# Constants folded into the small matrices, one read of the first batch, and a due time for every operation

## The chip, the cores and the metric

The kernel runs on one core of one Trainium2 chip. The metric is the device time of one execution in microseconds (us). The median of three runs is 2964.1 us (2961.46 to 2966.37).

## The reference, cut to what matters

Two batches of 12480 rows of 128 numbers go through an attention with 32 inducing rows, and then through two dense layers with a hidden width of 2048. All is float32; the weights arrive as float64 and are narrowed on the chip.

```python
def mab(q, kv):
    s = scale * (q @ kv.T);  a = exp(s - s.max(-1));  a /= a.sum(-1) + 1e-9
    return a @ kv
h   = mab(inducing, x)          # 32 x 128 per batch
x   = mab(x, h)                 # 24960 x 128 over both batches
h   = x @ w_in;  h2 = h*h;  h3 = h2*h                       # layer 1
g   = (a[0] + a[1]*h + a[2]*h2 + a[3]*h3) / (1 + |b[0]|*|h| + |b[1]|*h2 + 1e-6)
x   = g @ w_out
h   = x @ w_in2;  out = (h * cos(h)) @ w_out2               # layer 2
```

## The kernel before, in words

A batch is cut into 26 blocks of 480 rows, so there are 52 blocks. The last product of the attention, `a @ h`, is never formed: since a row of x after the attention is a row of `a` (32 numbers) times `h`, layer 1 multiplies `a` by `h @ w_in`, a small matrix that `plan_product` makes once per batch. To keep float32 precision in TensorE's faster float32r form, each small matrix is held as a rounded upper half and the rest (hi and lo). There are three of them for each of the eight tiles `k` of 256 hidden columns: `mst` (h @ w_in), `m3` (times a[3]) and `m1` (times a[1]).

Layer 1 of a tile (`moe1_tile`), for each of two halves of 128 hidden columns: `mmA` gives h; ScalarE takes `sq` (L859) and `ab` (L862); GpSimd makes the denominator with `wq` (L865) and `qq` (L868), over both halves at once; ScalarE takes `ln` (L871) and `ex` (L874), which is 1/Q; GpSimd's `ee` (L877) prepares a correction of it. For the numerator `mmX` writes a[3]*h into a PSUM bank; VectorE's `n1` (L883) adds a[2] and multiplies by h squared; `mmY` adds a[1]*h into the same bank; VectorE's `gr` (L891) adds a[0] and multiplies by 1/Q; `ng` (L896) applies the correction; `mmB` (L901) multiplies by `w_out`. `mmA`, `mmX` and `mmY` all show as L853.

Layer 2 (`moe2_tile`), sixteen times per block: `mmC` (L984), `rk` on ScalarE (L987, to an integer), `rd` on VectorE (L990), `sn` on ScalarE (L993, the sine), `gg` on VectorE (L996), `mmD` (L999). Layer 2 of a block runs while layer 1 of the next is under way. Logarithm and exponential live in one ScalarE table and the sine in another; `phases` lets the `ln`/`ex` of one block and the `sn` of the block before it alternate as wholes, with a table load between (L1079).

The order of the instructions on every engine is written out by a planner at build time. Each operation has a cost, dependencies, buffers to take and give back, and a priority; `Plan.order` simulates the engines and takes the ready operation with the lowest priority each time. Before, the priority is `16*block + slope*k` plus one offset for each kind of operation (`OFF`; `START` for the first two blocks).

Ahead of the blocks, `plan_attention` reads the rows of a batch twice from HBM, in 26 pieces of 240 KB each time: once to transpose them for the scores (L558, L498) and once for `a @ x` (L664), and it narrows the weights (`plan_narrow`, pieces of 384 columns): one ScalarE operation (L402), four VectorE ones (L406, L414, L420, L426) and three on GpSimd (L432, L436, L437), the last two a mask for values near zero. The attention of the second batch runs among the first two blocks; block 2 and later wait for all of it (`full`). Where the second batch begins (block 26), `plan_product` has to overwrite the small matrices of the first.

Of the kernel before, what the change touches and what calls it, by code (L numbers as in the profile page):

```python
# [21 lines left out]

OWN = {"act": 140.0, "dve": 115.0, "pool": 125.0}
HOPS = {("act", "dve"): 142.0, ("dve", "act"): 128.0, ("act", "pool"): 170.0}
# [5 lines left out]
    "ADDED": (0, 1, 2, 3, 4, 5, 6, 7),  # L30
    "OFF": {
# [12 lines left out]
        "mmY": -1100207.547, "mmB": 572.571, "mmC": 263.586, "mmD": 459.524, "sq": -1101114.205, "ab": 352.265, "ln":  # L44
        565.602, "ex": -1099842.388, "rk": 515.904, "sn": -1101113.631, "wq": -1099913.759, "qq": -177.405, "ee":
        -1100601.458, "wb": -1099292.294, "n0": -1099927.018, "n1": 356.455, "gr": -1099724.394, "ng": 299.344, "rd":
        -197.362, "gg": 1101720.214, "cpx": -57.339,
# [27 lines left out]
class Op:  # L75
    __slots__ = ("eng", "cost", "fn", "prio", "phase", "acq", "rel", "lat", "ndep", "users", "seq", "ready", "t0", "key", "main", "lock", "after", "inst", "tag", "deps")

    def __init__(self, eng, cost, fn, deps, prio, phase=None, acq=(), rel=(), lat=0.0, key=None, main=False, lock=None, tag=None):
        self.eng, self.cost, self.fn, self.prio = eng, cost, fn, prio
        self.phase, self.acq, self.rel, self.lat = phase, acq, rel, lat  # L80
        self.key, self.main, self.lock, self.tag = key, main, lock, tag
        self.users = []
        self.after = []
        self.inst = None
        self.ready = 0.0
        deps = [d for d in deps if d is not None]
        self.deps = deps
        self.ndep = len(deps)
        for d in deps:
            d.users.append(self)  # L90


class Plan:
# [3 lines left out]
    def __init__(self, pools, phases, switch=1300.0):  # L97
# [64 lines left out]
    def order(self):  # L162
# [6 lines left out]
        clock = Clock()  # L169
        events = []  # L170
# [13 lines left out]
        while events:  # L184
# [12 lines left out]
            for e in engines:  # L197
# [37 lines left out]
                if e == "pe":  # L235
                    cost = clock.run(now, cost)
# [23 lines left out]
def kernel(  # L260
# [19 lines left out]
    G = 4  # L280
# [8 lines left out]
    TINY = math.ldexp(1.125, -15) ** 2  # L289
# [3 lines left out]
    ROOM = [['xn', 'x1', 'xn', 'x1', 'x2', 'xn', 'x2'], ['xn']]  # L293
    PEPRIO = [0.0, 0]
    OFF, START = TUNE["OFF"], TUNE["START"]
    APRIO = [-1000000.0, OFF["ap1"]]
    WPRIO = [OFF["wp0"], OFF["wp1"], OFF["wp2"], OFF["wp3"]]
    ADDED = TUNE["ADDED"]
    PARTS = TUNE["PARTS"]
    NAT = 2  # L300
# [17 lines left out]
    m3 = {k: const.tile([128, 256], F32R, name=f"m3_{k}") for k in ADDED}  # L318
    m1 = {k: const.tile([128, 256], F32R, name=f"m1_{k}") for k in ADDED}
# [17 lines left out]
    plan = Plan({"slot": 3, "hc": TUNE["NX"]["hc"], "accB": 1, "accD": 1, "at": NAT, "xt": 2, "pk": 2, "ot": 1, "on": 2, "xn": NXN, **NX, "x1": NX["x1"] + 1, "x2": NX["x2"] + 1}, phases)  # L337
# [26 lines left out]
    XT = [t[:, 0:TB] for k in ("x5", "x6", "ot", "on") for t in M[k]]  # L364
    late = [(k, len(M[k])) for k in ("x5", "x6", "ot", "on")]
    for k, n in (("x3", 4), ("x2", 2)):
        late.append((k, n))
        XT += [M[k][i][:, h * TB:(h + 1) * TB] for i in range(n) for h in range(2)]
    XT = XT[:NQ]
# [27 lines left out]
    def plan_narrow(n, load, tiles, dst, prio, deps, acq=(), rel=()):  # L397


        def sq():  # L400
            raw, a, _ = tiles()
            nc.scalar.activation(out=a, in_=raw[:, :, 1].bitcast(F32), func=AF.Square)  # L402

        def mant():
            raw, _, _ = tiles()
            nc.vector.tensor_scalar(  # L406
                out=dst().bitcast(I32), in0=raw[:, :, 1], scalar1=0x07FFFFFF, scalar2=3,
                op0=ALU.bitwise_and, op1=ALU.logical_shift_left,
            )

        def top():
            raw, _, _ = tiles()
            d = dst().bitcast(I32)
            nc.vector.scalar_tensor_tensor(  # L414
                out=d, in0=raw[:, :, 1], scalar=-0x40000000, in1=d, op0=ALU.bitwise_and, op1=ALU.bitwise_or
            )

        def power():
            _, _, b = tiles()
# [4 lines left out]
        def rest():  # L424
            raw, _, b = tiles()
# [4 lines left out]
        def both():  # L430
            _, _, b = tiles()
# [9 lines left out]
        o1 = op("act", 94 + 0.833 * n, sq, [ld], prio, main=main)  # L441
        o2 = op("dve", 68 + 1.04 * n, mant, [ld], prio, main=main)
        for fn, t in ((top, 1.2), (power, 0.62), (rest, 1.12)):
            o2 = op("dve", 68 + t * n, fn, [o2], prio, main=main)
        o2 = op("pool", 95 + 2.16 * n, both, [o2], prio, main=main)
        return op("pool", 220 + 4.4 * n, keep, [o1, o2], prio, rel=rel, main=main)

    def plan_weights(w, out, dst, prio):

        ends = []  # L450
        for f in range(0, DFF, 384):
            n = min(384, DFF - f)
# [9 lines left out]
            def tiles(c=c, d=d, n=n):  # L462
                raw = M["x3"][c["x3"]][:, 0:2 * n].bitcast(I32).rearrange("p (n w) -> p n w", w=2)
                t = M["x1"][d["x1"]]
                return raw, t[:, 0:n], t[:, n:2 * n]
# [650 lines left out]
```

## Time and profile before

| | |
|---|---|
| median of three runs | 2964.1 us |
| the profiled execution | 2961.48 us, its span 2959.7 us |
| PE, DVE, ACT, POOL busy | 96%, 90%, 93%, 81% |
| granted clock of TensorE, mean | 0.985 |
| read from HBM, written | 33.97 MB, 12.78 MB |

A span is the time from the first to the last instruction. Engine names: PE is TensorE, DVE VectorE, ACT ScalarE, POOL GpSimd, SP the engine that issues the DMAs. L883 is line 883 of the kernel. An instruction's duration can overlap the next one's, so the distance of two starts (a slot) is often shorter than the duration.

### The profile page before, as it was taken

The page shows a single profiled execution, that of the slowest core. Times are in us where ns is not written, and L with a number is a line of the kernel's source. Part 1 is how long each engine was busy: PE and PEld are TensorE (multiplying, and loading weights), DVE is VectorE, ACT ScalarE, POOL GpSimd, SP SyncE. Part 2 cuts the span into 40 slices and gives each one's busy share as a digit, 9 for nine tenths or more (in the row PEclk, how much of TensorE's full clock was granted, in tenths as well). Part 3 has the DMA queues.
Part 4 walks back from the last instruction along what each step waited for, and adds up shares of the span by engine and source line. Part 5 has one row for each costly group of instructions (what it writes and reads, how often), then busy time and mean ns, then how long its engine had stood idle before and what let it go on. Part 6 is the DMA issues. An engine that isn't in the chain of part 4 may idle for free.

```text
span 2959.7 us, 31027 instructions
## 1 busy us (share of the span) xinstructions
PE 2837.3 (96%) x8903; PEld 1462.6 (49%) x8903; DVE 2654.1 (90%) x4444; ACT 2752.6 (93%) x4701; POOL 2390.8 (81%) x1392
## 2 busy tenths in 40 slices
PE   6789999999999999999989999999999999999999
PEld 3345455554555545555444455454554545545454
DVE  6889999899998999989989989899898998989987
ACT  3689999999999999999989999999999999999995
POOL 5799788787887878878768878788787887878871
PEclk8789999999999999999999999999999999999999
DMA  9420000000000000000000000000000000000000
GB/s 252 136 74 4 4 7 4 7 4 4 7 4 7 4 4 7 4 8 4 4 7 4 4 7 4 4 7 4 7 4 4 7 4 7 4 4 7 4 7 7
DMA packets 27585, 48.75 MB, mean 16 GB/s; under 512 B 3028, under 2 KB 7412, under 8 KB 27412
## 3 DMA queue, kind: packets, MB, share of 16 engines
q1 hardware_dynamic: 27412, 46.76, 5.7%
q8 instruction: 70, 1.15, 0.2%
q14 instruction: 103, 0.84, 0.1%
HBM read 33.97 MB, written 12.78 MB: 16 GB/s over the span
## 4 chain that ended last, share of the span: by engine, by line
PE 70%; DVE 20%; ACT 5%; issue 3%; DMA 1%; POOL 1%; SPq 0%; DVEq 0%; ACTq 0%; POOLq 0%
PE acc L999 20%; PE bank L984 17%; PE bank L853 16%; PE acc L901 14%; DVE bank L891 5%; DVE x L896 5%; DVE bank L883 4%; DVE x L990 3%; PE bank L1025 1%; DVE x L996 1%; ACT x L871 1%; ACT x L874 1%; PE bank L812 1%; DMA x<-in_moe_w_in_dram 1%; ACT x L987 1%
## 5 line engine op out<-in xcount | busy, mean ns | idle before, releaser
L877 POOL TENSOR_TENSOR x<-x,x 128x960 f32<-128x960 f32 x315 | 703.6, 2250 | 360.7 <-ACT x L874 360.1
L853 PE MATMUL bank<-at,m 128*128 128x480 f32 x1664 | 775.8, 521 | 12.1 <-DVE x L896 4.1
L883 DVE SCALAR_TENSOR_TENSOR bank<-bank,par,x 128x480 f32<-128x480 f32 x832 | 592.5, 720 | 205.8 <-PE bank L853 195.8
L984 PE MATMUL bank<-xt,wt 128*128 128x480 f32 x1664 | 746.9, 571 | 0.3 <-ACT xt L957 0.2
L999 PE MATMUL acc<-x,wt 128*128 128x480 f32 x1664 | 744.8, 566 | 0.0
L868 POOL TENSOR_TENSOR x<-x,x 128x960 f32<-128x960 f32 x315 | 705.3, 2246 | 4.8 <-ACT x L862 3.9
L901 PE MATMUL acc<-x,wout 128*128 128x480 f32 x1460 | 703.7, 569 | 0.0
L993 ACT ACTIVATE x<-x 128x480 f32<-128x480 f32 x832 | 487.5, 614 | 59.5 <-DVE x L990 53.3
L990 DVE TENSOR_TENSOR x<-x,bank 128x480 f32<-128x480 int32 x832 | 524.9, 646 | 14.5 <-ACT x L987 11.7
L996 DVE TENSOR_TENSOR x<-x,bank 128x480 f32<-128x480 f32 x832 | 518.3, 648 | 10.9 <-PE acc L999 1.7
L891 DVE SCALAR_TENSOR_TENSOR bank<-bank,par,x 128x480 f32<-128x480 f32 x716 | 503.7, 717 | 11.4 <-PE bank L853 10.1
L987 ACT ACTIVATE x<-bank 128x480 int32<-128x480 f32 x832 | 465.7, 599 | 25.7 <-PE bank L984 23.8
L853 PEld LDWEIGHTS bank<-at,m 128*128 128x128 f32 x1664 | 307.4, 190 | 351.5 <-DVE bank L883 121.3
L859 ACT ACTIVATE x<-bank 128x480 f32<-128x480 f32 x832 | 448.6, 594 | 21.9 <-PE bank L853 17.1
L862 ACT ACTIVATE x<-bank,babs 128x480 f32<-128x480 f32 x730 | 465.7, 700 | 0.0
L984 PEld LDWEIGHTS bank<-xt,wt 128*128 128x128 f32 x1664 | 302.9, 189 | 324.9 <-issue 143.2
L896 DVE SCALAR_TENSOR_TENSOR x<-x,bank 128x480 f32<-128x480 f32 x730 | 458.7, 645 | 5.2 <-POOL x L877 1.1
L999 PEld LDWEIGHTS acc<-x,wt 128*128 128x128 f32 x1664 | 315.4, 190 | 276.1 <-issue 255.0
L853 PE MATMUL bank<-at,mst 128*128 128x480 f32 x832 | 375.0, 492 | 54.6 <-DVE x L896 46.5
L865 POOL TENSOR_SCALAR x<-x,babs 128x960 f32<-128x960 f32 x358 | 384.3, 1081 | 15.7 <-ACT x L859 15.5
L874 ACT ACTIVATE x<-x 128x960 f32<-128x960 f32 x358 | 358.9, 1043 | 0.2
L871 ACT ACTIVATE x<-x 128x960 f32<-128x960 f32 x315 | 319.1, 1035 | 3.3 <-POOL x L868 2.8
(125 smaller groups left out, 2415.2 us busy)
## 6 DMA issues: line engine op xcount, KB each, us to landing
wide<-in_x_dram SPq DMA_DIRECT2D x75, 240.0 KB, 3.9
out_dram<-on SPq DMA_DIRECT2D x52, 240.0 KB, 2.4
x<-in_x_dram SPq DMA_DIRECT2D x29, 240.0 KB, 7.8
x<-in_moe_w_in_dram SPq DMA_DIRECT2D x10, 384.0 KB, 6.5
x<-in_moe_w_out_dram SPq DMA_DIRECT2D x10, 384.0 KB, 5.1
x<-in_moe_w_in_dram SPq DMA_DIRECT2D x2, 128.0 KB, 4.3
x<-in_moe_w_out_dram SPq DMA_DIRECT2D x2, 128.0 KB, 4.2
ind<-in_inducing_dram SPq DMA_DIRECT2D x1, 16.0 KB, 1.6
```

What stands on the lines that cost most here:

```text
L853: return nc.tensor.matmul(out=ps(e), lhsT=m[k][:, h * 128:(h + 1) * 128], rhs=M["at"][at["at"]], **flags)
L868: nc.gpsimd.tensor_tensor(out=fl("x1"), in0=fl("x2"), in1=fl("x1"), op=ALU.add)
L877: nc.gpsimd.tensor_tensor(out=fl("x1"), in0=fl("x1"), in1=fl("x2"), op=ALU.mult)
L883: nc.vector.scalar_tensor_tensor(out=ps(cx[h]), in0=ps(cx[h]), scalar=par[:, 2:3], in1=hf("x3", h), op0=ALU.add, op1=ALU.mult)
L891: nc.vector.scalar_tensor_tensor(out=ps(cx[h]), in0=ps(cx[h]), scalar=par[:, 0:1], in1=hf("x2", h), op0=ALU.add, op1=ALU.mult)
L896: nc.vector.scalar_tensor_tensor(out=hf("x1", h), in0=hf("x1", h), scalar=-2.0, in1=ps(cx[h]), op0=ALU.add, op1=ALU.mult)
L901: nc.tensor.matmul(out=acc[0][:, 0:TB], lhsT=wout1[:, (2 * k + h) * C:(2 * k + h + 1) * C], rhs=hf("x1", h), start=(k == 0 and h == 0), st ...
L984: return nc.tensor.matmul(out=ps(), lhsT=win2[:, f * 128:(f + 1) * 128], rhs=M["xt"][xc["xt"]], start=True, stop=True)
L987: nc.scalar.activation(out=fl("x5").bitcast(I32), in_=ps(), func=AF.Identity, bias=0.25)
L990: nc.vector.tensor_tensor(out=fl("x5"), in0=fl("x5").bitcast(I32), in1=ps(), op=ALU.subtract)
L996: return nc.vector.tensor_tensor(out=fl("x6"), in0=fl("x5"), in1=ps(), op=ALU.mult)
L999: nc.tensor.matmul(out=acc[1][:, 0:TB], lhsT=wout2[:, f * C:(f + 1) * C], rhs=fl("x6"), start=first, stop=last)
```

## The change

Five things change. (1) `a[2]` and `a[0]` are added to the entries of `m3` and `m1` when these are made (the weights of an attention row sum to one), so `n1` and `gr` become plain products. The product is made twice per tile, once for `mst` and once for `m3` and `m1`, and the two wait for different predecessors; the lower halves of `m3` and `m1` are made on POOL. (2) The rows of batch 0 are read once, 15 pieces of 7 rows per partition, into buffers of layer 1, and serve both passes. (3) Weights are narrowed in 32 pieces of 256 columns, without the two mask operations; the last addition is on DVE. The weights of layer 2 are loaded into buffers that come free after batch 0's second pass. [...] (5) The copies of the attention weights (`cpe`) move from DVE to ACT.

```diff
+    def due(blk, name, i=0, early=0.0):
+        if blk < 2 and name in START:
+            return START[name] + START["block"] * blk + START["tile"] * i * (1.0 if name in SINGLE else 0.5)
+        return PERIOD * blk + TAU[f"{name}{i}"] + ATT["origin"] - early
...
         def n1(h):
-            nc.vector.scalar_tensor_tensor(
-                out=ps(cx[h]), in0=ps(cx[h]), scalar=par[:, 2:3], in1=hf("x3", h), op0=ALU.add, op1=ALU.mult
-            )
+            return nc.vector.tensor_tensor(out=ps(cx[h]), in0=ps(cx[h]), in1=hf("x3", h), op=ALU.mult)
...
         def gr(h):
-            nc.vector.scalar_tensor_tensor(
-                out=ps(cx[h]), in0=ps(cx[h]), scalar=par[:, 0:1], in1=hf("x2", h), op0=ALU.add, op1=ALU.mult
-            )
+            nc.vector.tensor_tensor(out=ps(cx[h]), in0=ps(cx[h]), in1=hf("x2", h), op=ALU.mult)
...
-    def plan_product(b, k, oh, p, ends):
+    def plan_product(b, k, oh, p, ends, stage):
-        before = [blocks[b * NQ - 1][n][k] for n in ("rA", "rX", "rY") if k in blocks[b * NQ - 1][n]] if b else []
+        prev = blocks[b * NQ - 1] if b else {}
+        before = [prev[n][k] for n in (("rA",) if stage == 0 else ("rX", "rY")) if prev]
...
-        def hj(m, s):
-            nc.scalar.activation(out=m, in_=bank[c["half"]][:, 0:256], func=AF.Identity, scale=s)
-        def lj(m, s):
-            return nc.vector.scalar_tensor_tensor(
-                out=m[64:128], in0=bank[c["half"]][64:128, 0:256], scalar=s[64:128], in1=m[64:128].bitcast(F32),
-                op0=ALU.mult, op1=ALU.subtract,
-            )
+        def line(i):
+            if ON["line"] == "act":
+                return nc.scalar.activation(
+                    out=whole[i], in_=bank[c["half"]][:, 0:256], func=AF.Identity, scale=par[:, 3 - 2 * i:4 - 2 * i],
+                    bias=par[:, 2 - 2 * i:3 - 2 * i],
+                )
+        def hj(i):
+            nc.scalar.activation(out=(m3, m1)[i][k], in_=whole[i], func=AF.Copy)
+        def lj(i):
+            m = (m3, m1)[i][k]
+            nc.gpsimd.tensor_tensor(out=m[64:128], in0=whole[i][64:128], in1=m[64:128].bitcast(F32), op=ALU.subtract)
...
+        if b == 0:
+            for i, (k, t) in enumerate(NATURAL):
+                n = min(LG, NJ - LG * i)
+                if n > 0:
+                    dst = M[k][t][:TP, 0:n * C].rearrange("p (g c) -> p g c", g=n)
+                    def ld(dst=dst, i=i, n=n):
+                        nc.sync.dma_start(out=dst, in_=xv[:, LG * i:LG * i + n, :])
...
         def both():
-            _, _, b = tiles()
-            nc.gpsimd.tensor_tensor(out=b, in0=dst(), in1=b, op=ALU.add)
-        def keep():
-            _, a, b = tiles()
-            nc.gpsimd.tensor_scalar(out=a, in0=a, scalar1=TINY, scalar2=None, op0=ALU.is_ge)
-            nc.gpsimd.tensor_tensor(out=dst(), in0=a, in1=b, op=ALU.mult)
+            _, b = tiles()
+            return (nc.vector if on == "dve" else nc.gpsimd).tensor_tensor(out=dst(), in0=dst(), in1=b, op=ALU.add)
...
-            smax.append(op("dve", 68 + 125 * n, mxr, [scopy[-1], state["st"]], p))
+            scopy.append(op("act", 52 + 100 * n, scp, [o1, *(narrowed if b else [])], p, rel=[("half", c)]))
```

## Rows read from the trace of the kernel before

**Rows 1.** The page's first part: busy time, share of the span, instructions.
```profile
PE 2837.3 (96%) x8903; PEld 1462.6 (49%) x8903; DVE 2654.1 (90%) x4444; ACT 2752.6 (93%) x4701; POOL 2390.8 (81%) x1392
```

**Rows 2.** The chain of waits in order of time: start, length, what.
```profile
1421.59 6.44 PE acc L999 x16
...
1635.54 0.65 PE bank L853 x3
...
1652.96 6.44 PE acc L999 x16
...
1705.79 6.44 PE acc L999 x16
```

**Rows 3.** Busy time in one stretch: length, busy of each engine, clock.
```profile
1692.32:1745.15 52.83, 51.84 (x154) 26.74 (x153) 48.30 (x82) 51.41 (x89) 44.31 (x26) 1.00 0.02 5
```

**Rows 4.** ACT's instructions in time (start, busy), inside the same stretch.
```profile
1697.58 1.14 ACT L993 ACTIVATE x<-x 128x480 f32<-128x480 f32 x2
1698.57 0.61 ACT L987 ACTIVATE x<-bank 128x480 int32<-128x480 f32 x1
...
1719.63 1.07 ACT L859 ACTIVATE x<-bank 128x480 f32<-128x480 f32 x2
1720.53 1.27 ACT L862 ACTIVATE x<-bank,babs 128x480 f32<-128x480 f32 x2
1721.62 1.08 ACT L871 ACTIVATE x<-x 128x960 f32<-128x960 f32 x1
1722.51 0.65 ACT L859 ACTIVATE x<-bank 128x480 f32<-128x480 f32 x1
```

**Rows 5.** Groups of instructions, 1600 to 2600 us: busy, mean ns, idle before.
```profile
L883 DVE SCALAR_TENSOR_TENSOR bank<-bank,par,x 128x480 f32<-128x480 f32 x304 | 217.0, 720 | 75.8 <-PE bank L853 71.7
L990 DVE TENSOR_TENSOR x<-x,bank 128x480 f32<-128x480 int32 x301 | 189.8, 646 | 1.3 <-ACT x L987 0.3
L891 DVE SCALAR_TENSOR_TENSOR bank<-bank,par,x 128x480 f32<-128x480 f32 x260 | 182.7, 717 | 3.3 <-PE bank L853 2.9
L993 ACT ACTIVATE x<-x 128x480 f32<-128x480 f32 x300 | 175.5, 614 | 21.0 <-DVE x L990 18.7
L896 DVE SCALAR_TENSOR_TENSOR x<-x,bank 128x480 f32<-128x480 f32 x266 | 167.0, 645 | 1.3
L1079 ACT ACT_TABLE_LOAD x38 | 48.8, 1283 | 0.7
```

**Rows 6.** Groups of instructions, 1440 to 1600 us, around the batch's change.
```profile
L768 DVE SCALAR_TENSOR_TENSOR m<-bank,par,m 64x256 fp32r<-64x256 f32 x16 | 7.8, 491 | 4.2 <-ACT m L765 4.0
L765 ACT ACTIVATE m<-bank,par 128x256 fp32r<-128x256 f32 x16 | 7.5, 492 | 1.5 <-DVE m L768 1.5
...
L760 DVE TENSOR_TENSOR mst<-bank,mst 64x256 fp32r<-64x256 f32 x8 | 3.4, 428 | 0.1
L757 ACT ACTIVATE mst<-bank 128x256 fp32r<-128x256 f32 x8 | 3.2, 432 | 0.0
```

**Rows 7.** Busy time in the first stretch; the last three columns: clock, DMA share, GB/s.
```profile
0.00:80.50 80.50, 48.16 (x412) 27.36 (x412) 48.77 (x98) 27.42 (x57) 43.87 (x50) 0.81 0.93 250
```

**Rows 8.** The chain of waits from 0 to 130 us.
```profile
25.93 7.86 DMA x<-in_x_dram
...
46.11 0.17 DVE st L591
...
80.46 0.21 DVE hp L677
```

**Rows 9.** The page's DMA issues: count, KB each, median us to landing.
```profile
wide<-in_x_dram SPq DMA_DIRECT2D x75, 240.0 KB, 3.9
...
x<-in_x_dram SPq DMA_DIRECT2D x29, 240.0 KB, 7.8
```

**Rows 10.** Groups of instructions that narrow the weights, 0 to 240 us.
```profile
L436 POOL TENSOR_SCALAR x<-x 128x384 f32<-128x384 f32 x20 | 23.7, 1186 | 1.7
...
L426 DVE SCALAR_TENSOR_TENSOR x<-x,x 128x384 f32<-128x384 uint32 x20 | 14.6, 732 | 0.4
...
L414 DVE SCALAR_TENSOR_TENSOR wt<-x,wt 128x384 int32<-128x384 int32 x10 | 5.5, 551 | 0.1
```

More of the change, by code (lines that the diff above doesn't have):

```diff
@@ L235, in order @@
                 if e == "pe":
-                    cost = clock.run(now, cost)
+                    cost = clock.run(now, cost + (WAKE if cost and now > busy[e] + 1.0 else 0.0))
+                if o.port:
+                    cost += max(0.0, port["pool" if e == "dve" else "dve"] - now)
+                    port[e] = now + cost
                 for pool, holder, ordered in o.acq:
@@ L519, in plan_turn, with plan_attention @@
         return c, op("pe", 105.0 * n, tr, deps, prio, acq=[("half", c, False)])
-    state = {"xT": [[] for _ in range(NQ)], "st": None}
-    def plan_attention(b, prio, first, room, ends):
+    state = {"xT": {}, "st": None, "hm": None}
+    def plan_attention(b, prio, ends):
         xv = x[b].rearrange("(p j) c -> p j c", j=NJ)
@@ L671, in plan_attention @@
                 prev = op(
-                    "pe", 585, hm, [ens[gi], ol, prev], nxt() + first, acq=[] if prev else [("half", ch, False)],
-                    rel=[(room[(NQ + q) % len(room)], xc)],
-                )
+                    "pe", 585, hm, [ens[gi], *landed[NQ + q], prev], nxt(), acq=[] if prev else [("half", ch, False)],
+                    rel=frees[NQ + q] + (natural if b == 0 and q == NQ - 1 else []),
+                )
+        if b == 0:
+            state["xT"] = {("x2", i, h): [prev] for i in range(2) for h in range(2)}
         def h1():
@@ L774, in plan_product @@
[L774 to L786 removed]
+        def line(i):
[3 more added lines that the diff above has]
+                    bias=par[:, 2 - 2 * i:3 - 2 * i],
+                )
+            return nc.vector.tensor_scalar(
+                out=whole[i], in0=bank[c["half"]][:, 0:256], scalar1=par[:, 3 - 2 * i:4 - 2 * i],
+                scalar2=par[:, 2 - 2 * i:3 - 2 * i], op0=ALU.mult, op1=ALU.add,
+            )
@@ L788, with move @@
+        products[b, k, stage] = done
+    MOVE = {"act": 452.0, "dve": 566.0}
+    def move(eng, out, src, by=None):
+        if eng == "act":
+            return nc.scalar.activation(out=out, in_=src, func=AF.Copy, scale=1.0 if by is None else by)
+        if by is None:
+            return nc.vector.tensor_copy(out=out, in_=src)
+        return nc.vector.tensor_scalar(out=out, in0=src, scalar1=by, scalar2=None, op0=ALU.mult)
     ov = out.rearrange("(b p q g) c -> b p q g c", b=NB, p=TP, q=NQ)
@@ L836, in moe1_tile, with pri @@
         ac = blkd.setdefault("acc1", {})
-        off = table(blk)
-        base = 16.0 * blk + off["slope1"] * k
-        def pri(name, h=0):
-            return base + off[name] + 0.01 * h
+        def pri(name, h=None):
+            return due(blk, name, k if h is None else 2 * k + h)
         def ps(e):
@@ L1020, in cpo @@
             def cpo():
-                nc.scalar.activation(out=M["ot"][oc["ot"]], in_=acc[1][:, 0:TB], func=AF.Copy, scale=TWO_PI)
+                return move(ON["cpo"], M["ot"][oc["ot"]], acc[1][:, 0:TB], TWO_PI)
             def tro():
@@ L1062 @@
                 for k in range(NT):
-                    plan_product(s // NQ, k, ready_h[s // NQ], 16.0 * s - 8.0 + OFF["slope1"] * k, win1_ends)
-            start_block(s, 16.0 * s - 16.0)
+                    for stage in range(2):
+                        plan_product(s // NQ, k, ready_h[s // NQ], due(s, "mmX" if stage else "mmA", 2 * k, ATT[f"early{stage}"]), win1_ends, stage)
+            start_block(s)
             for k in range(NT):
```

326 lines of the change are left out of this document (169 added, 157 removed), and 61 rows, old and new, of the table TUNE.

## The prediction, made before the changed kernel was run

> **What bounds the kernel now.** I read the page's busy times first [rows 1]: PE 96%, ACT 93%, DVE 90%, POOL 81%. Four engines this close together mean that no single share tells the limit, and the page warns that a busy PE is not PE at its peak. So I went to the chain of waits, in order of time, to find the period [rows 2]. The run of 16 L999 matmuls that closes layer 2 comes back at 1652.96 and 1705.79 us: a block takes 52.83 us. One matmul of that run takes 6.44 / 16 = 0.4025 us, and three L853 in a row 0.65, so 0.217 each. A block has 96 of the first kind (48 float32 matmuls in two parts each) and 48 of the second: 38.6 + 10.4 = 49.0 us, and about 1 us more for eight transposes (an estimate, from the same rate). PE could do a block in some 50 us; it loses nearly 3 of 52.83.
>
> Then the busy time of exactly one period [rows 3]: PE 51.84, ACT 51.41, DVE 48.30, POOL 44.31. ACT is idle for only 1.42 us. To see how far ACT could go, I took slots (start to start) from its instructions in time [rows 4]: `sn` 0.495 (two in 0.99), `sq` 0.45, `ab` 0.545, `ln` 0.89. With `rk` at the 0.45 of `sq` and `ex` at the 0.89 of `ln` (estimates: same shapes), a block holds 16 x (0.45 + 0.545 + 0.45 + 0.495) + 16 x 0.89 + two table loads of 1.28 [rows 5] + five small copies of about 0.45 = 31.0 + 14.2 + 2.6 + 2.2 = 50.1 us. That is ACT's floor; its busy time of 51.41 holds another 1.3 us of gaps too short to be shown as idle.
>
> Last, what waits for what in the steady part [rows 5]. In the 1000 us from 1600 on, which are 18.9 periods, the `n1` of L883 found DVE idle for 75.8 us, 4.0 per period, nearly all until PE's L853. That is the change of phase: `mmX` needs the first `ex`, which needs the table load and two `ln`. Outside this gap DVE has work all the time, and PE loses its 3 us behind it. So the cycle is: ACT changes tables, DVE stands still for 4 us, then DVE works off 48 us. 48.3 + 4.0 + 0.5 is the period. **DVE with its gap sets the period today, and ACT stands 1.4 us behind it.**
>
> **The change, part by part.** The sum is made against the profiled execution's own 2961.48 us (span 2959.7 and 1.8 around it), which is 2.6 below the median of the three runs.
>
> *Plain products for `n1` and `gr`.* 32 instructions per block lose their scalar. They take 720 and 717 ns now [rows 5]. `rd`, a plain product or difference of the same shape, takes 646, and `ng`, the same three-operand form as `n1` but with a number in place of a column of `par`, takes 645. So it is not the form that costs 72 to 74 ns; it is either the scalar from `par` or the write into a bank, which only `n1` and `gr` do. The instructions around the batch's change tell which [rows 6]: L768 (a scalar from `par`) takes 491, L760 (none) 428, both writing to SBUF. 63 of the 72 to 74 ns are the scalar. 32 x 0.065 = 2.1 us per block. The ends are 0.3 (if only the 9 ns that L768 does not show were saved) and 2.4; I take 2.1, by the nearest rows.
>
> [...]
>
> *The order by due times.* With DVE at 46.2 and the same gap, the period would be 52.83 - 2.1 = 50.7. But ACT's instructions in a steady block stay the same, so ACT becomes the limit: 50.1 by slots, 51.41 by its busy time now. What is late next is ACT, with PE (50) right behind, and two engines that depend on each other do not both run without gaps. I take 51.3: ACT keeps its busy time and loses nearly all of its 1.42 us of idle. That is 1.53 us in each of 50 steps (52 blocks have 51 steps, of which the last is only the end of layer 2): **-76 us**. Ends: 50.5 (-116) and 52.8 (0).
>
> *The batch's change.* From 1421.59 to 1652.96 are four blocks [rows 2]: 231.4 - 4 x 52.83 = 20.1 us more than four steady ones. The new product in two stages lets block 26's `mmA` start when `mst` alone is new. It adds 8 products on PE (of 256 columns, some 0.45 each by the rate above, 3.6 us) and 16 copies on ACT, and moves 16 L768 of 0.491 from DVE to POOL. ACT then has 8 x 0.432 (L757) + 16 x 0.492 (L765, for `line`) + 16 x 0.432 (the new copies, priced as L757) = 18.2 us of busy time, against 11.3 now [rows 6]. Slots being shorter than durations, some 15 us stay, and ACT is where they cannot hide. 20 to 15: **-5 us**. Ends -9 and +5, the latter if all 18.2 are added and a gap remains.
>
> *The first batch's rows read once.* In the first 80.5 us the DMA share is 0.93 and 250 GB/s move [rows 7], 20 MB. Of the 104 pieces of 240 KB [rows 9] 52 are batch 0's, 12.8 MB; one reading is 6.4 MB, 26 us at that rate. Today the first reading's last piece lands at 33.8 us, the maxima are done at 46.1, and the second reading's result is copied at 80.5 [rows 8]. With the rows first in the queue and landed by about 29 us, the maxima are done at 29 + 12.3 = 41. The rest took 34.3 us under the second reading; without it, it takes something between 0 and 34.3. I take half, so the copy comes at 58 instead of 80.5, 22 us earlier. Behind it come the second batch's 52 pieces and layer 2's weights on the same SP queue; they are moved past nothing but the first batch's rows, and they too start earlier. [...]
>
> *The weights without a mask.* POOL loses two of three operations on each piece, the mask's L436 being 1.19 us of it [rows 10]. DVE gains 32 additions; at the 0.55 of the 384-wide L414 that is at most 18 us, less the 7.9 us of L768 that go to POOL. Its cover is DVE's idle time, 31.7 of the first 80.5 us [rows 7]. If that cover is gone, the 10 us stand on the path. Of the 22 us gained I therefore take **-18 us**; ends -39 and +15.
>
> One row speaks against this part. L426 and L414 have the same shape and two SBUF inputs each, but L426 takes 732 ns on average and L414 551 [rows 10]; L426 is the one whose neighbours in time are POOL's operations on the same piece. [...]
>
> Sum: 2961.5 - 76 - 18 - 5 = **2862 us**.
>
> **The rivals.**
>
> *ACT's floor is reached.* For it: ACT's slots sum to 50.1, and DVE and PE fit beside it. Against it: PE has only 0.5 us to spare at such a period. 50.5 gives -116, with -30 at the start and -6 at the batch's change: 2809.
>
> *The products cost what they did.* If the bank write is the price, or the length alone counts, DVE keeps its 48.3 and its gap, and the period stays at 52.8. For it: all other DVE instructions of 645 ns write to SBUF. Against it: L768 and L760. What remains is -18 and -5: 2938.
>
> *DVE loses the start to POOL.* If each of the 160 operations that narrow the weights (five in each of 32 pieces) pays the 181 ns between L426 and L414, DVE has 29 us more at the start and the -18 become +11: 2891.
>
> *Slower: ACT waits for DVE in the sine phase.* `sn` waits for `rd`, and that is the largest wait ACT has: 21.0 us in 18.9 periods, 1.1 each [rows 5]. ACT takes its instructions in the written order, so whatever stands behind a waiting `sn` (the next `rk`, `sq`, `ln`) is late too, and PE behind it. A due time for each operation can put an `n1` or `gr` in front of a needed `rd`. With ACT's busy time at 51.41, its idle time decides: 1.42 now, and the 23 us gained at the start and at the batch's change are used up once it passes 1.42 + 23 / 50 = 1.9. Two of the 16 `sn` that wait for one more DVE instruction each (0.565 us, an estimate from the 646 ns less its overlap) give 2.5: 53.9, so +54 - 23 = 2993. Against it: DVE has 2.1 us less to do.
>
> **How the numbers follow.** My forecast has 0.60, with 2825 to 2905 as its own range (period 50.9 to 52.0). ACT's floor has 0.10, the unchanged price 0.12, the lost start 0.08, the slower order 0.10. The time predicted is 2862 us. 2805 to 2945 leaves out the slower case and the edges of the first two rivals, about 0.2. Against about 0.2% (6 us), what a measurement of this kernel can tell: faster 0.60 + 0.10 + 0.10 + 0.08 = 0.88; same 0.03, from the edges of the unchanged price and of the slower case; slower 0.09.
>
> **What would show it.** The steps, in the changed kernel's profile: the mean of `n1` and `gr` near 650 ns; DVE busy near 46 us of a period; the period, by the run of 16 L999's successors, near 51.3, with ACT's idle below 0.5 us; four blocks around the batch's change within 15 us of four steady ones; HBM reads down by 6.4 MB and the copy of the second pass's result near 58 us. I am wrong if the period stays above 52.3 with `n1` shorter (then PE or ACT, not DVE, set it), or if the first `mmA` does not come earlier.

## The result, and the profile after

The changed kernel takes 2875.32 us (median of 4 runs, 2873.48 to 2876.15), the kernel before 2963.91 beside it: a ratio of 0.97 [0.9683, 0.9717]. The forecast was 2862 us, 13 below it, and the time lies in the range (2805 to 2945, and the forecast's own 2825 to 2905). The profiled execution has a span of 2873.5 us, 86.2 less than before.

The page's busy times, as in [rows 1], and its line on memory:

```profile
PE 2788.5 (97%) x8935; PEld 1500.0 (52%) x8935; DVE 2565.0 (89%) x4462; ACT 2752.7 (96%) x4755; POOL 2346.1 (82%) x1352
...
HBM read 27.58 MB, written 12.78 MB: 14 GB/s over the span
```

The reads fell from 33.97 to 27.58 MB, one reading of the first batch. The chain of waits in order of time (start, length, what), as in [rows 2]:

```profile
1386.14 5.63 PE acc L1083 x14
...
1607.20 5.63 PE acc L1083 x14
...
1709.73 5.63 PE acc L1083 x14
...
1760.81 5.63 PE acc L1083 x14
```

L1083 is `mmD`, L999 before. A steady block takes 51.08 us instead of 52.83 (51.44 once in a while). The four blocks around the batch's change take 1607.20 - 1386.14 = 221.06, which is 221.06 - 4 x 51.13 = 16.5 more than four steady ones (51.13 is the mean of the steady stretches below); before it was 20.1. One steady block's busy times, as in [rows 3]:

```profile
1709.73:1760.81 51.08, 50.87 (x153) 27.53 (x153) 46.93 (x80) 50.96 (x89) 44.39 (x25) 1.00 0.02 5
```

PE and ACT show 0.2 us of idle or less. DVE has 4.15 us, nearly the 4.53 of before [rows 3]. The groups of 1600 to 2600 us, as in [rows 5]: `n1` is L978, `gr` L984, `gg` L1080, `sn` L1077; the first line is `gg` before.

```profile
L996 DVE TENSOR_TENSOR x<-x,bank 128x480 f32<-128x480 f32 x302 | 188.1, 648 | 3.8 <-ACT x L993 0.3 <-PE acc L999 0.2
...
L1080 DVE TENSOR_TENSOR x<-x,bank 128x480 f32<-128x480 f32 x314 | 198.9, 648 | 31.8 <-PE acc L1083 27.7
L978 DVE TENSOR_TENSOR bank<-bank,x 128x480 f32<-128x480 f32 x314 | 197.8, 659 | 23.7 <-PE bank L948 23.5
L1077 ACT ACTIVATE x<-x 128x480 f32<-128x480 f32 x313 | 187.4, 630 | 0.2
L957 ACT ACTIVATE x<-bank,babs 128x480 f32<-128x480 f32 x272 | 182.0, 705 | 0.0
L954 ACT ACTIVATE x<-bank 128x480 f32<-128x480 f32 x312 | 176.8, 610 | 0.0
L984 DVE TENSOR_TENSOR bank<-bank,x 128x480 f32<-128x480 f32 x272 | 175.5, 659 | 2.8 <-PE bank L948 0.8
```

Four things to see: `n1` and `gr` cost 659 ns each; the idle before `n1` fell from 75.8 to 23.7 us; most of it is not gone but stands elsewhere, ahead of `gg` (3.8 before, now 31.8) above all; and ACT no longer waits ahead of `sn` (21.0 before, now 0.2).

Where the 86.2 us came from, counted from block to block at the copy that ends a block's layer 2 (ACT, `ot<-acc`), differences of the two traces:

| stretch | before | after | difference |
|---|---|---|---|
| start to the end of block 1 | 322.0 | 325.6 | +3.6 |
| 21 blocks to block 22 | 1110.1 | 1073.0 | -37.1 |
| four blocks around the batch's change | 231.4 | 221.1 | -10.3 |
| 22 blocks to block 48 | 1162.4 | 1125.8 | -36.6 |
| block 48 to the end of the span | 133.8 | 128.0 | -5.8 |

(The copy follows a block's last `mmD` at different distances. By the end of that `mmD` the first line is +5.0 and the last -7.2.) So the steady blocks gave 37.1 + 36.6, of the 10.3 another 4 x 1.7, and the last stretch, which is the rest of the blocks, 5.8: some 86 us. The batch's change gave 3.6. **The start lost some 4 us, where a gain of 18 was forecast.**

### The profile page after: what moved, and what is told of

Read it like the earlier page. It is cut to its first block, busy times and chain, and to the rows that moved or that the text cites. A ratio compares the mean times of both kernels' runs of the same rounds, so it can differ in the third digit from the quotient of the medians.

```text
span 2873.5 us, 31081 instructions
## 1 busy us (share of the span) xinstructions
PE 2788.5 (97%) x8935; PEld 1500.0 (52%) x8935; DVE 2565.0 (89%) x4462; ACT 2752.7 (96%) x4755; POOL 2346.1 (82%) x1352
## 3 DMA queue, kind: packets, MB, share of 16 engines
HBM read 27.58 MB, written 12.78 MB: 14 GB/s over the span
## 4 chain that ended last, share of the span: by engine, by line
PE 78%; DVE 12%; ACT 4%; issue 3%; DMA 2%; POOL 1%; SPq 0%; DVEq 0%; ACTq 0%; POOLq 0%
PE bank L1068 23%; PE acc L992 21%; PE acc L1083 18%; PE bank L948 14%; DVE bank L978 6%; DVE bank L984 3%; DVE x L987 2%; DMA wide<-in_x_dram 1%; PE bank L1109 1%; PE bank L909 1%; ACT x L954 1%; ACT x L957 1%; ACT whole L847 1%; DMA x<-in_x_dram 0%; POOL x L972 0%
## 5 line engine op out<-in xcount | busy, mean ns | idle before, releaser
L972 POOL TENSOR_TENSOR x<-x,x 128x960 f32<-128x960 f32 x364 | 818.0, 2253 | 311.3 <-ACT x L969 311.1
L963 POOL TENSOR_TENSOR x<-x,x 128x960 f32<-128x960 f32 x364 | 813.1, 2246 | 0.7
L1083 PE MATMUL acc<-x,wt 128*128 128x480 f32 x1664 | 745.5, 566 | 0.1
L992 PE MATMUL acc<-x,wout 128*128 128x480 f32 x1460 | 689.2, 576 | 9.3 <-DVE x L987 8.4
L1080 DVE TENSOR_TENSOR x<-x,bank 128x480 f32<-128x480 f32 x832 | 526.0, 648 | 79.2 <-PE acc L1083 67.2
L978 DVE TENSOR_TENSOR bank<-bank,x 128x480 f32<-128x480 f32 x832 | 524.8, 659 | 77.1 <-PE bank L948 76.3
L1077 ACT ACTIVATE x<-x 128x480 f32<-128x480 f32 x832 | 497.2, 628 | 7.1 <-DVE x L1074 6.4
L1071 ACT ACTIVATE x<-bank 128x480 int32<-128x480 f32 x832 | 482.8, 608 | 14.8 <-PE bank L1068 11.2
L957 ACT ACTIVATE x<-bank,babs 128x480 f32<-128x480 f32 x730 | 487.5, 705 | 0.0
L954 ACT ACTIVATE x<-bank 128x480 f32<-128x480 f32 x832 | 471.3, 609 | 16.0 <-PE bank L948 16.0
L984 DVE TENSOR_TENSOR bank<-bank,x 128x480 f32<-128x480 f32 x730 | 471.4, 659 | 12.7 <-PE bank L948 6.3
L1083 PEld LDWEIGHTS acc<-x,wt 128*128 128x128 f32 x1664 | 315.1, 190 | 277.5 <-issue 244.4
L969 ACT ACTIVATE x<-x 128x960 f32<-128x960 f32 x365 | 383.0, 1049 | 0.4
L966 ACT ACTIVATE x<-x 128x960 f32<-128x960 f32 x364 | 374.3, 1041 | 9.2 <-POOL x L963 8.6
L948 PE MATMUL bank<-at,mst 128*128 128x480 f32 x832 | 366.3, 492 | 3.2 <-ACT x L957 1.8
```

The source lines that it names most:

```text
L948: return nc.tensor.matmul(out=ps(e), lhsT=m[k][:, h * 128:(h + 1) * 128], rhs=M["at"][at["at"]], **flags)
L957: nc.scalar.activation(out=hf("x1", h), in_=ps(ca[h]), func=AF.Abs, scale=babs[:, 0:1])
L963: nc.gpsimd.tensor_tensor(out=fl("x1"), in0=fl("x2"), in1=fl("x1"), op=ALU.add)
L972: nc.gpsimd.tensor_tensor(out=fl("x1"), in0=fl("x1"), in1=fl("x2"), op=ALU.mult)
L978: return nc.vector.tensor_tensor(out=ps(cx[h]), in0=ps(cx[h]), in1=hf("x3", h), op=ALU.mult)
L984: nc.vector.tensor_tensor(out=ps(cx[h]), in0=ps(cx[h]), in1=hf("x2", h), op=ALU.mult)
```

## The experiments: the steady blocks

The periods below are the mean over the 21 blocks from block 1 to block 22, at the same copy. Time ratios are to the kernel before.

**Price back, order kept.**

```diff
-            return nc.vector.tensor_tensor(out=ps(cx[h]), in0=ps(cx[h]), in1=hf("x3", h), op=ALU.mult)
+            return nc.vector.scalar_tensor_tensor(
+                out=ps(cx[h]), in0=ps(cx[h]), scalar=par[:, 6:7], in1=hf("x3", h), op0=ALU.add, op1=ALU.mult
+            )   # par[:, 6:7] is zero; gr likewise
```

> The changed kernel in its own order, but the product steps n1 and gr on VectorE go back to the three-operand form, with a column of zeros as the scalar (so the result is the same and only the price comes back: 16 x 63 + 16 x 69 ns = 2.1 us of VectorE per block). My theory: in the steady blocks TensorE (50.87 us busy of 51.08) and ScalarE (50.96) are both full and VectorE has 4.15 us of idle per block, so most of the 2.1 us is taken from that idle: 2875 to 2900 us. Rival: the chain TensorE, n1, mmY, gr runs through VectorE, so the price comes back in full, 50 blocks x 2.1 us: 2975 to 2985 us.

Measured: 2935.71 us, ratio 0.9903 [0.9888, 0.9919], 60 us above the changed kernel; the period is 52.35. Neither end held. VectorE's groups, 1600 to 2600 us:

```profile
L979 DVE SCALAR_TENSOR_TENSOR bank<-bank,par,x 128x480 f32<-128x480 f32 x306 | 209.3, 718 | 22.3 <-PE bank L949 22.3
...
L987 DVE SCALAR_TENSOR_TENSOR bank<-bank,par,x 128x480 f32<-128x480 f32 x267 | 188.4, 718 | 0.5
```

The same instructions in the same places take 718 ns again, so the column of `par` is the price, 59 ns each and 16 x 2 x 59 = 1.9 us per block. 1.26 us of it come back in the period although VectorE had 4.15 us of idle: its idle time is not where its work is late. The line that shows it is PE's, ahead of `mmX` and `mmY`, which find PE idle for 13.6 us in the 1000 (4.8 in the changed kernel), 10.6 of them until VectorE's `ng` (L992):

```profile
L949 PE MATMUL bank<-at,m 128*128 128x480 f32 x615 | 282.8, 516 | 13.6 <-DVE x L992 10.6 <-DVE bank L979 1.5
```

**Price away, old order.**

```diff
-                out=ps(cx[h]), in0=ps(cx[h]), scalar=par[:, 2:3], in1=hf("x3", h), op0=ALU.add, op1=ALU.mult
+            return nc.vector.tensor_tensor(out=ps(cx[h]), in0=ps(cx[h]), in1=hf("x3", h), op=ALU.mult)   # gr likewise
```

> The kernel before in its own order, with n1 and gr as plain two-operand products (this leaves out the added constants a2 and a0 and keeps all else: second read, masks, order). The price alone, 2.1 us of VectorE per block, in the old order. In the new order the same price was worth 1.23 us per block (52.35 against 51.12). Theory: price and order are nearly separate, so about the same here: 2964 - 50 x 1.2 = 2904 us, 2890 to 2915. Rival 1 (in the old order VectorE with its gaps sets the period, so the price comes off in full until ScalarE's 51.4 us holds): 2964 - 50 x 1.4 to 2.1 = 2860 to 2894 us. Rival 2 (the old order cannot use it): 2945 to 2964 us.

Measured: 2957.86 us, ratio 0.9986 [0.9976, 0.9996]; the period is 52.82 against 52.86. The old order could not use it. VectorE's groups in the same stretch:

```profile
L883 DVE TENSOR_TENSOR bank<-bank,x 128x480 f32<-128x480 f32 x304 | 198.8, 660 | 90.0 <-PE bank L853 87.7
...
L889 DVE TENSOR_TENSOR bank<-bank,x 128x480 f32<-128x480 f32 x260 | 169.5, 659 | 9.6 <-PE bank L853 7.4
```

`n1` is 60 ns shorter, and 14.2 us more of idle stand ahead of it, 6.3 ahead of `gr`, put down to `mmX` and `mmY`. Beside [rows 5] this reads: VectorE finished sooner and then waited for PE. Its work and gap together are not what sets the period there.

**Old due times, all else new.**

```diff
-        return PERIOD * blk + TAU[f"{name}{i}"] + ATT["origin"] - early
+        return old(blk, name, i) - early    # 16*blk + slope*k + OFF[name], as before
```

> The changed kernel with the constants in the matrices and all that is new in the start, but from block 2 on the planner takes the due times of the kernel before (an offset per kind of operation in place of one due time per operation). Theory: the period is 52.85 - 1.2 (price) = 51.6 us, so the new due times are worth some 0.5 us per block: 2875 + 48 x 0.5 = 2899 us, 2890 to 2915. Rival (the due times do nothing, all is the price): 2870 to 2880 us. Rival (the old rule falls into a worse pattern with the new costs): above 2925 us.

Measured: 3000.25 us, ratio 1.0127 [1.0112, 1.0143], period 53.45. The last rival held: a new plan by the old rule is worse than the old plan, though `n1` costs 658 ns in it. The idle ahead of `n1`:

```profile
L1001 DVE TENSOR_TENSOR bank<-bank,x 128x480 f32<-128x480 f32 x298 | 191.0, 658 | 70.3 <-PE bank L971 69.4 <-issue 0.2
```

It is the 70 to 90 us of every kernel with the old rule, against 22 to 24 with the new one. The offsets in this run are those of the kernel before, not fitted anew to the planner's changed costs; how far the old rule would come with fitted ones, no run shows. The four periods together:

| | price 718 ns | price 659 ns |
|---|---|---|
| old order | 52.86 | 52.82 |
| new order | 52.35 | 51.09 |

The price alone gives 0.04 us per block, the order alone 0.51, and both 1.77. The order by due times (one for each operation and tile from block 2 on, 50.5 us from block to block) makes room for the price.

**What bounds the block now.** Three kernels in the changed kernel's order:

```diff
-            nc.scalar.activation(out=hf("x1", h), in_=ps(ca[h]), func=AF.Abs, scale=babs[:, 0:1])
+            nc.scalar.activation(out=hf("x1", h), in_=ps(ca[h]), func=AF.Abs, scale=1.0)
```

> The changed kernel in its own order; the absolute value on ScalarE takes an immediate scale of 1.0 instead of the column of |b0| (this leaves out the factor |b0|). The same engine's square on the same shape takes 610 ns and the absolute value 705 ns, so ScalarE loses 16 x 0.095 = 1.5 us of work per block; TensorE keeps its 50.87 us. My theory (both engines full): almost nothing, 2865 to 2876 us. Rival (ScalarE alone sets the period and TensorE's busy time holds slack): 2875 - 48 x 1.5 = 2803 us.

```diff
-            return mm(cx[h], m1, h, start=False, stop=True, skip_group_check=True)
+            return nc.tensor.matmul(out=ps(cx[h])[:, 0:TB // 2], lhsT=m1[k][:, h * 128:(h + 1) * 128],
+                rhs=M["at"][at["at"]][:, 0:G // 2], start=False, stop=True, skip_group_check=True)
```

> The changed kernel in its own order; the second matmul into the gate's bank (mmY) runs on 240 of its 480 columns (this leaves out its term for half of the rows). TensorE loses some 16 x 0.2 to 0.26 us = 3.2 to 4.1 us of work per block; ScalarE keeps its 50.96 us of 51.08. My theory (both full): 2860 to 2876 us, the period stays at ScalarE's 50.9 us. Rival (TensorE alone sets the period, ScalarE's busy time is stretched by waiting on banks): 2875 - 48 x 3.2 = 2720 us at the least load, and anything below 2840 speaks for it.

> The two edits before it in one kernel (the factor |b0| and half of mmY left out), same order. If the period is the larger of TensorE's and ScalarE's work, it falls by ScalarE's 1.5 us per block: 2875 - 48 x 1.5 = 2803 us. If the written order or the hand-overs between the engines set it, it stays within 10 us of the better of the two single edits.

Measured: 2869.29 us (ratio 0.9677 [0.966, 0.9694]), 2868.94 (0.9678 [0.9663, 0.9693]) and 2844.92 (0.9596 [0.9581, 0.9612]); periods 51.03, 50.96 and 50.52. Either edit alone gives 6 us, as the theory for each had it. Both together give 30: neither the 72 of the sum by ScalarE's work nor a time within 10 us of the better single edit, as the rival had it. Busy times of PE, PEld, DVE, ACT and POOL in one stretch of ten blocks, in the changed kernel, then in these three in their order:

```profile
1709.00:2222.00 513.00, 510.69 (x1525) 275.58 (x1523) 470.03 (x802) 511.29 (x874) 443.68 (x250) 1.00 0.02 5
```
```profile
1709.00:2222.00 513.00, 509.55 (x1527) 276.76 (x1526) 470.07 (x803) 504.18 (x874) 443.90 (x251) 1.00 0.02 5
```
```profile
1709.00:2222.00 513.00, 509.79 (x1528) 265.50 (x1527) 472.26 (x804) 511.84 (x874) 443.29 (x250) 1.00 0.02 5
```
```profile
1709.00:2222.00 513.00, 508.29 (x1544) 264.72 (x1544) 473.91 (x813) 506.83 (x884) 450.60 (x255) 1.00 0.02 5
```

With ScalarE's work cut its idle grows from 1.7 to 8.8 us and the period stays: by the busy times, PE holds it. With PE's work cut, ScalarE stays full and the period stays: ScalarE holds it. With both cut both have some slack and the period falls by 0.57. So two engines bound the block together, since the pair of cuts is worth more than the sum of the two. Of the 1.5 us expected for ScalarE 0.57 arrive; whether the hand-overs or the written order keep the rest, no run shows. VectorE belongs to the bound too, although it is the least full of the three: with the price back, 1.9 us more of its work cost 1.26 in the same order.

## The experiments: the start

**The second reading back.**

```diff
+            if b == 0:
+                for i, (k, t) in enumerate(NATURAL):
+                    ...
+                    nc.sync.dma_start(out=M[k][t][:TP, 0:n * C]..., in_=xv[:, LG * i:LG * i + n, :])
             nc.vector.tensor_reduce(out=stat[0], in_=mx[:, 0:NG], axis=AX.X, op=ALU.max)
```

> The changed kernel in its own order, but the first batch's rows are read a second time into the same buffers after the maxima, as before the change (6.4 MB, some 25 us of transfers at 250 GB/s), and the pooling matmuls use that second read. Theory: the copy of the pooled row goes from 59.8 back to 78 to 90 us, and yet little of it reaches the end, since the products of tiles 0 to 2 come at 116 us anyway: 2875 to 2885 us. Rival (the earlier row is worth its 18 us and something else in the new start costs as much): 2888 to 2900 us.

Measured: 2893.36 us, ratio 0.9769 [0.9754, 0.9783], 18.0 us above the changed kernel. My theory fell and the rival held. The pooled row's copy `hp` (two batches: min, median, max ns, first and last start) and GpSimd's first `wq` (its first start), first in the kernel before:

```profile
L677 DVE COPY hp<-bank x2: 276/278/280, 80.4 to 185.9; 128x128 f32<-128x128 f32 x2
...
L865 POOL TENSOR_SCALAR x<-x,babs x26: 1059/1071/1438, 128.0 to 294.2; 128x960 f32<-128x960 f32 x26
```

then in the changed kernel:

```profile
L754 DVE COPY hp<-bank x2: 281/286/292, 59.8 to 158.8; 128x128 f32<-128x128 f32 x2
...
L960 POOL TENSOR_SCALAR x<-x,babs x25: 1057/1066/1310, 134.3 to 299.3; 128x960 f32<-128x960 f32 x25
```

and with the second reading back:

```profile
L761 DVE COPY hp<-bank x2: 275/278/281, 77.8 to 179.2; 128x128 f32<-128x128 f32 x2
...
L967 POOL TENSOR_SCALAR x<-x,babs x22: 1055/1064/1302, 152.2 to 296.8; 128x960 f32<-128x960 f32 x22
```

All of it moves by 18 to 20 us: `hp` by 18.0, `wq` by 17.9, the end of block 1 by 20.0 (345.6 against 325.6), the time by 18.0. So reading once is worth 18 to 20 us at the end, where the forecast counted 22 for it and took 4 off for the added work on VectorE. What ate them is the way from `hp` to the first `wq`: 47.6 us before, 74.5 now, 26.9 longer. From there to the first change to the sine table (the first start of the table loads from 200 us on, before and after) it is 108.4 and 105.9, nearly the same:

```profile
L1079 ACT ACT_TABLE_LOAD  x4: 1283/1283/1283, 236.4 to 313.5; - x4
```
```profile
L1166 ACT ACT_TABLE_LOAD  x4: 1283/1283/1283, 240.2 to 313.7; - x4
```

The 26.9 us have two parts. The first `mmA` starts at 125.4 us before and at 124.3 now, so from `hp` to it there are 19.5 us more (45.0 and 64.5), and from it to `wq` 7.4 more (2.6 and 10.0):

```profile
L853 PE MATMUL bank<-at,mst x89: 375/480/1335, 125.4 to 399.4; 128*128 128x480 f32 x89
...
L948 PE MATMUL bank<-at,mst x90: 373/386/1268, 124.3 to 398.8; 128*128 128x480 f32 x90
```

The second part can be read from the trace. Between the first `mmA` and the first `sq` ScalarE works off exponentials of the second batch's scores (L696, before L622) and copies of them (L705, which change (5) moved to ScalarE), with 0.26 us of idle time in 7.7. In the kernel before the last of these exponentials came at 154.5 us, behind the start of layer 1; now the last comes at 131.3, ahead of the first `sq` at 132.05:

```profile
L622 ACT ACTIVATE att<-att,st x14: 481/680/695, 48.1 to 154.5; 128x480 f32<-128x480 f32 x12, 128x240 f32<-128x240 f32 x2
...
L696 ACT ACTIVATE att<-att,st x14: 487/682/695, 41.0 to 131.3; 128x480 f32<-128x480 f32 x12, 128x240 f32<-128x240 f32 x2
...
132.05 0.56 ACT L954 ACTIVATE x<-bank 128x480 f32<-128x480 f32 x1
```

**Layer 1's first tiles first.** The pieces of `w_in` go from tile 0 up, with other due times for blocks 0 and 1 (numbers in `START` and `ATT`).

```diff
-        for f in range(0, DFF, n):
+        for f in (range(DFF - n, -1, -n) if home == "cv" and not out else range(0, DFF, n)):
```

> The changed kernel, but the pieces of the first in-matrix are read and narrowed from tile 0 up and not from tile 7 down, with other due times for the blocks 0 and 1 and the attention, so that the order stays free of deadlock; GpSimd's first layer-1 operation should fall from 134.3 us to about 100. Theory (GpSimd's 16 tiles x 5.5 us = 88 us, counted from that operation, end the start): the end of block 1's layer 2 falls from 325.6 to some 295 to 305 us, the kernel to 2845 to 2860 us. Rival (the second batch's scores, softmax and the narrowing of the layer-2 weights hold ScalarE and VectorE until 194 us whatever GpSimd does, and GpSimd gets gaps instead): block 1 ends within 8 us of 325.6, 2867 to 2885 us.

Measured: 2884.12 us, ratio 0.9733 [0.9717, 0.9749], 9 us slower than the changed kernel; block 1 ends at 336.1. The time lies in the rival's range, the end of block 1 in neither.

```profile
L748 DVE COPY hp<-bank x2: 273/276/278, 60.7 to 175.5; 128x128 f32<-128x128 f32 x2
...
L954 POOL TENSOR_SCALAR x<-x,babs x23: 1056/1066/1352, 100.6 to 297.8; 128x960 f32<-128x960 f32 x23
```

The first `wq` came at 100.6, 34 us earlier, and the theory that the start ends 88 us of GpSimd's work after it fell: the second batch's `hp` came 17 us later (175.5 against 158.8), and between 134 and 240 us GpSimd was busy for 80 us, 94 in the changed kernel (the changed kernel first; after the stretch's length, GpSimd's busy time, the clock, the DMA share and GB/s):

```profile
134.00:240.00 106.00, 93.76 (x56) 0.84 0.14 42
```
```profile
134.00:240.00 106.00, 79.98 (x50) 0.84 0.21 62
```

**What lies in the 26.9 us.** Two loads taken out, singly and together, in the changed kernel's order. In the chain of waits the changed kernel's way to the last products (`h @ w_in` of tiles 0 to 2, L832) runs through two transfers:

```profile
98.97 5.52 DMA wide<-in_x_dram
...
108.66 5.01 DMA x<-in_moe_w_out_dram
...
116.68 2.02 PE bank L832 x4
```

```diff
+            if n == 256 and acq[0][0] == "x1":     # layer 2's pieces: in shift, mant, top, power, rest, both
+                return None
```

> The changed kernel in its own order, but the 16 pieces of the two layer-2 matrices are read and not narrowed (a constant stands in for them): some 18 us of VectorE and 4 us of ScalarE go from 62 to 134 us, and with them VectorE's queue ahead of the last pieces of the first in-matrix. Theory (that queue is what stretches the way from the pooled row to GpSimd's first layer-1 operation from 47.6 to 74.5 us): that operation comes at 114 to 122 us and not 134.3, and the kernel ends 10 to 16 us earlier, 2859 to 2866 us. Rival (the matrices' transfers, the second batch's transposes or the buffers hold it): first operation after 130 us, 2871 to 2876 us.

```diff
-                        out=M["xn"][c["xn"]].rearrange("p (g c) -> p g c", g=G), in_=xv[:, q * G:(q + 1) * G, :]
+                        out=M["xn"][c["xn"]][:, 0:m * C]..., in_=xv[:, q * G:q * G + m, :]   # m = 1 in the first pass
```

> The changed kernel in its own order, but the second batch's first pass reads 60 of each 240 KB (this leaves out three quarters of its rows in the scores), so 4.8 MB fewer stand in the queue between 64 and 105 us. In the changed kernel the chain from 96 to 117 us runs through two transfers, a piece of the second batch's rows (5.5 us) and one of layer 2's weights (5.0), while in the kernel before these rows were read after GpSimd had begun layer 1. Theory (the second batch's rows, moved ahead of the last products, hold GpSimd's first layer-1 operation together with the layer-2 weights): that operation comes 6 to 14 us earlier than 134.3, and so does the end: 2861 to 2869 us. Rival (the transfers hide behind VectorE's narrowing, 18 us of work in the same stretch): 2872 to 2876 us.

> Both edits at the start in one kernel: a quarter of the second batch's rows in its first pass, and the layer-2 matrices read and not narrowed (the latter alone gave 125.6 us for GpSimd's first layer-1 operation and 9.6 us at the end). Theory (rows and narrowing together are the 26.9 us by which the way from the pooled row to that operation became longer): it comes at 105 to 113 us, the end at 2846 to 2855 us. Rival (something else, such as the order of the products itself, holds the rest): it stays at 118 us or later, the end at 2858 us or more.

Measured: 2865.76 us (ratio 0.9673 [0.9658, 0.9687]), 2873.3 (0.9697 [0.9682, 0.9711]) and 2864.88 (0.9666 [0.965, 0.9682]); the first `wq` at 125.6, 133.7 and 125.2. Narrowing layer 2's weights is worth 8.7 us at the first `wq` and 9.6 at the end: the end lies in the theory's range, the first `wq` between theory and rival. These weights did not move in time. Their narrowing starts with L406 before and with L464 now:

```profile
L406 DVE TENSOR_SCALAR wt<-x x12: 216/372/1142, 66.0 to 139.6; 128x384 int32<-128x384 int32 x10, 128x128 int32<-128x128 int32 x2
...
L464 DVE TENSOR_SCALAR wt<-x x16: 278/282/821, 67.2 to 137.8; 128x256 int32<-128x256 int32 x16
```

It is `hp` that now comes ahead of them: 7 of 12 pieces began between `hp` and the first `wq` before, 15 of 16 do now. How much of the 9 us the kernel before paid too, no run shows.

The rows' transfer is worth next to nothing: the rival held both times, and the 5.5 us in the chain are a transfer that had another wait right behind it. (In the two kernels with short reads `hp` itself came later, at 62.3 and 61.1 us; from `hp` to `wq` they are 3 and 1 us shorter than the kernels they are compared with.) With both gone, the chain from 95 to 99 us is this:

```profile
95.38 0.67 DVE x L657
...
97.38 1.01 PE bank L567 x8
98.40 0.57 PE bank L648 x4
```

L648 and L657 transpose the second batch's rows and copy them, L567 makes its scores: this is the second batch's first pass, which the new order puts ahead of the last three products. How much of the way it is worth, no run took out.

**The additions on GpSimd again.**

```diff
-            return (nc.vector if on == "dve" else nc.gpsimd).tensor_tensor(out=dst(), in0=dst(), in1=b, op=ALU.add)
+            return (nc.gpsimd if add.t0 < 112000.0 else nc.vector).tensor_tensor(out=dst(), in0=dst(), in1=b, op=ALU.add)
```

> The changed kernel in its own order, but the last step of each narrowed piece (the addition) that is planned before 112 us goes from VectorE to GpSimd, as in the kernel before; GpSimd is idle for 80% of that stretch and for all of 100 to 120 us. It takes 26 x 0.41 us off VectorE, some 5 us of them between 62 and 113 us, at 0.6 to 0.7 us each on GpSimd. Theory (VectorE's queue stretches the start): the end comes 3 to 5 us earlier, 2870 to 2872 us. Rival (the piece's chain gets longer by the slower addition and two hand-overs, and VectorE waits for it): 2875 to 2885 us.

Measured: 2874.5 us, ratio 0.9705 [0.9688, 0.9721], the first `wq` at 135.3: no difference from the changed kernel, and neither range holds it. But VectorE was not relieved. Up to 134 us it has some 26 instructions less and is busy for only 1.2 us less, where 26 additions of 0.41 are 10.7 (the changed kernel first; after the length VectorE's busy time and its instructions, the clock, the DMA share and GB/s):

```profile
0.00:134.00 134.00, 89.70 (x246) 0.87 0.64 174
```
```profile
0.00:134.00 134.00, 88.52 (x219) 0.87 0.63 172
```

What it saved went into others of its operations, which took longer beside GpSimd's additions. L478 had 281 ns in the first 62 us of the changed kernel and has 418 here:

```profile
L478 DVE TENSOR_SCALAR att<-wout 128x256 int32<-128x256 int32 x8 | 3.3, 418 | 0.3
```

So this run does not tell what a lighter VectorE would be worth.

## Why the prediction came out as it did

The total is only 13 us off because the 22 us that are missing at the start (18 forecast, 4 lost) are partly made up by some 10 more than forecast from the steady blocks. That the two errors have opposite signs is luck.

*The products' price: right.* -61 and -58 ns against the 65 taken; with a bank at both ends they take 659 ns, 11 more than the 648 of L1080, which has one at one end. At the same length and between the same banks the form with the column takes 718 and the plain product 659, so the length alone does not set the time.

*The steady blocks: the size right (-76, measured some -86 with the blocks of the end), the reason half wrong.* "DVE with its gap sets the period today" is refuted by the price taken away in the old order: `n1` was shorter and the period stayed above 52.3, which the text had named (for the changed kernel) as the sign that PE or ACT set it. The gap ahead of `n1` goes with the old rule, in which `mmX` comes late; under the new order DVE has as much idle time as before in other places. What brings the gain is the new order together with the price. That ACT becomes the limit is half right: ACT and PE do, each holding the other's saving. What in the old order sets 52.8, ACT's 51.4 us or the hand-overs, was not taken apart.

*The batch's change: -5 forecast, -3.6 measured.* Four blocks around it take 16.5 us more than four steady ones, where the text wanted 15. No run took this apart.

*The start: the step that failed.* "Of the 22 us gained I therefore take **-18 us**" has two parts. The gain came: `hp` at 59.8, forecast 58, and one reading is worth 18 to 20 us at the end. The text then let everything behind `hp` move up with it: the second batch's pieces and layer 2's weights "are moved past nothing but the first batch's rows". But they were moved past more. 26.9 us more lie between `hp` and layer 1's first denominator, and the first `mmA`, which the text wanted earlier as a sign of being right, comes 1.1 us earlier where `hp` comes 20.6 earlier. With the narrowing of layer 2's weights left out the way is 9 us shorter. Some 17 are left. 7.4 of them are, by the trace, the second batch's exponentials and copies on ScalarE between the first `mmA` and the first `sq`. In the rest the second batch's first pass stands in the chain, which is argued and not shown. With the first tiles put first the 17 vanish (`hp` to `wq` 40.0) and come back later as GpSimd's waits and a late second batch. Whether an order exists that keeps both stays open.

*The rivals.* "DVE loses the start to POOL" came nearer to the start than the forecast (+11, measured some +4), but by another way. The prices it took, 181 ns on 160 operations, did not come, for the change had taken most of GpSimd's work away there (34.4 us busy in the first 62 before). In the first 62 us, with GpSimd busy for 0.7 us, and from 62 to 114, with GpSimd busy for 17.5:

```profile
L484 DVE SCALAR_TENSOR_TENSOR att<-att 128x256 f32<-128x256 uint32 x12 | 5.0, 417 | 0.1
...
L478 DVE TENSOR_SCALAR att<-wout 128x256 int32<-128x256 int32 x8 | 2.2, 281 | 0.0
```
```profile
L484 DVE SCALAR_TENSOR_TENSOR x<-x 128x256 f32<-128x256 uint32 x8 | 3.7, 465 | 0.0
L478 DVE TENSOR_SCALAR x<-wt 128x256 int32<-128x256 int32 x9 | 3.4, 381 | 0.0
```

48 and 100 ns on some 45 operations are 2 to 4.5 us. With the additions back on GpSimd (busy for 9.4 of the first 62 us) L478 pays 137 there: the rival's price is real where GpSimd has work beside it. L478, which has one input, pays more (100 ns) than L484, which has two (48 ns), and no run here shows why.

## What to carry to other kernels

Idle time on an engine says that its work could be shorter or later, not that it sets the period: take the price away in the old order (0.04 us per block here) before counting on it. Where a change shortens a first step and rewrites the order behind it, sum both (here 20.6 us earlier at `hp` and 26.9 more behind it): the gain is real only as far as the steps behind it keep their distance. And where two engines are full, the worth of a cut is found only by cutting both (here 6 us for either, 30 for both).

## What the runs showed of the hardware

PE's busy time hardly fell when its work did. With `mmY` on half its columns PE is busy for 509.8 of 513 us, against 510.7; `mmA`, which was not touched, is longer instead. The first line is the changed kernel's `mmA` (min, median, max ns), the second that kernel's:

```profile
L948 PE MATMUL bank<-at,mst x312: 375/382/761, 1614.6 to 2599.0; 128*128 128x480 f32 x156
```
```profile
L948 PE MATMUL bank<-at,mst x314: 372/475/761, 1613.2 to 2597.6; 128*128 128x480 f32 x157
```

The durations lie in groups, most of them near 380, 480 and 755 ns, so the median jumps from 382 to 475 where the mean goes from 485 to 501. The same matmul's duration thus changes with what runs around it, by 16 ns in the mean (I read this as waiting that is not shown as idle), and it does not tell what the cut took off. By the 0.217 us of one L853 [rows 2], half of a `mmY` is some 0.11 us, 1.7 per block (an estimate), and not the 3.2 that I had expected, which counted a whole `mmY`.

On ScalarE, too, a duration changed without an edit. With an immediate scale the absolute value fell from 705 to 588 ns, and the square beside it, not touched, from 610 to 572:

```profile
L954 ACT ACTIVATE x<-bank 128x480 f32<-128x480 f32 x314 | 168.3, 572 | 8.0 <-PE bank L948 3.9
L957 ACT ACTIVATE x<-bank 128x480 f32<-128x480 f32 x274 | 153.0, 588 | 0.0
```

Some 80 of the 117 ns are thus the column of per-partition numbers (an estimate, by the square's 38), as 59 are on VectorE (718 against 659).
